# Routing scratch moved out of the logits' bank, first queries loaded by halves, and weight splits moved between engines in a retention and mixture-of-experts kernel

## The chip, the cores and the metric

One core of one Trainium2 chip runs the whole program. The metric is device time in microseconds of one execution: the median of three runs. Lower is better. TensorE is called PE below (PEld is its loading of weights), VectorE DVE, ScalarE ACT, GpSimd POOL and SyncE SP.

## What is computed

Attention with a decaying state, for 4 batches, 8 heads, 768 positions and 64 columns a head, feeds a mixture of 8 experts of which each token takes the best one. Cut to what matters:

```python
gamma = 1.0 - 2.0 ** (-5.0 - np.arange(H))
for t in range(S):
    state = gamma[None, :, None, None] * state + np.einsum('bhd,bhe->bhde', k[:, :, t], v[:, :, t])
    y[:, :, t] = scale * np.einsum('bhd,bhde->bhe', q[:, :, t], state)
x = y.transpose(0, 2, 1, 3).reshape(B * S, H * D)             # 3072 tokens of 512
logits = x @ w_gate;  e_idx = np.argmax(logits, axis=1)
gate_w = softmax(logits)[np.arange(N), e_idx]
eom = 1.0 / (1.0 + np.exp(-(x @ w_output_gate)))
for e in range(E):
    mask = e_idx == e
    h = np.maximum(x[mask] @ w1[e], 0.0)                      # 512 -> 1024
    out[mask] = gate_w[mask, None] * eom[mask, e, None] * (h @ w2[e])
```

## The kernel before

The order of the work on every engine is written out by hand (`manual_schedule`), so each engine executes what the program's lines issue to it, in their order; the framework adds only the waits.

**Attention.** The sequences are cut into 24 chunks of 128 positions, and two chunks (of two batches) make a pair `p`, 0 to 11. Within a pair PE makes, in this order: the products with the state (`inter`), the scores of both chunks into four banks of PSUM (`sp[0]` to `sp[3]`, each 128 x 512), the tokens of the chunks two pairs back (`tokens`, into `sp[0]` and `sp[1]`), the turned logits of the pair before, a turn of queries into `sp[0]`, the values into `yp`, the new state into `st`, the turned keys of the next pair (`turn_keys`, into `sp[2]` and `sp[3]`), the `counts` of the pair before, a second turn of queries into `sp[1]`, and the `logits` of this pair into `misc`. DVE masks the scores, scales the outputs into `yt` and does the small operations of the routing; ACT copies keys, queries, state and logits out of PSUM (`keep_keys`, `keep_queries`, `keep_logits`), takes exponentials and makes the output rows (`rows_out`); POOL scales the values (`prep_v`) and scatters the rows to the experts' regions in memory (`srt`). Loads run on SP's queue.

**Routing.** `route1` (eight DVE operations) gets the best expert `oh` from the turned logits, `exps` its exponentials, `counts` (five small products) how many tokens of each expert came earlier, `route2` the row number `pos` and `gates` the factor `gate`, by which `rows_out` multiplies two pairs later. The counts stand in `misc[:, 2 * P:]` and the scratch of all these steps in `small`, a part of the same bank; the logits of the pair are written to `misc[:, 0:2 * P]`.

**Start.** Queries are loaded for two chunks at once (`load_q`, 512 KB, rows of both parities side by side), parted by a copy for each parity (`part_queries`), turned, and copied to `qt`. `warm_up` gives PE products that nobody reads. The tables `gn` and `ga` of the decay and the values of chunk 0 go over ACT's queue, the four pieces of the gate weights `wg` over SP's.

**Head.** The expert with most tokens is chosen from pair 7 on; its first 256 rows are computed early, as a stream of 192 products (`head_all`: stage 1 of tile 0, then stage 1 of tile f and stage 2 of tile f - 1, twelve each, for eight tiles). `run_head(n)` puts the next n of them into PE's order. Weights are split into a high and a low part for each tile: `split_high` (two ACT casts), `split_low` (two halves, the first on DVE and the second on POOL unless said otherwise). `head_prep` turns and splits the first rows. At the end of the stream stands `begin_x0`, which takes the expert's remaining rows; they are loaded (`load_x`) when the last scatter and a clearing of unused rows (`clear`) have landed.

**Experts.** From there on PE runs the eight experts, with their weights loaded, split and used in a row of 64 tiles.

Of the kernel before, what the change touches and what calls it, by code (L numbers as in the profile page):

```python
# [10 lines left out]
F32 = mybir.dt.float32  # L11
# [22 lines left out]
def retention_moe_kernel(  # L34
# [167 lines left out]

    def split_weights(s: int):
        split_high(s)
        split_low(s)
# [25 lines left out]
    with ExitStack() as actx:  # L231
# [59 lines left out]
        load_q(0, 0)  # L291
        load_k(0)
        nc.scalar.activation(warm, warm, AF.Exp)
        nc.scalar.dma_start(gv, dec_v)
        load_v(0, nc.scalar)
        for o in range(2):
            nc.scalar.dma_start(gn[rows(o)].rearrange("p (b s) t -> p b (s t)", b=2),
                                dec_q[:, 2 * o * P:2 * o * P + 2 * P].unsqueeze(0).broadcast_to([HP, 2, 2 * P]))
        nc.scalar.dma_start(ga.rearrange("p b c g -> p (b c g)"),
                            dec_c.rearrange("b x -> (b x)").unsqueeze(0).broadcast_to([P, 2 * NC * NG]))  # L300
        load_k(1)
        load_q(1, 0)
        load_v(1)
        load_k(2)
        load_k(3)
        load_v(2)
        for o in range(2):
            for x, w in ((0, w_gate), (E, w_ogate)):
                nc.sync.dma_start(wg[rows(o), :, x:x + E],
                                  w[o * DM // 2:(o + 1) * DM // 2].rearrange("(g p) e -> p g e", p=HP))  # L310
        load_v(3)
        load_q(0, 1)

# [23 lines left out]
        def turn_queries(ch, j, r, bank):  # L337
            src = qr.pop((ch, j, r))
            for g in range(NG):
                nc.tensor.transpose(blocks(bank)[:, g], src[:, 2 * g:2 * g + 2].rearrange("p h d -> p (h d)"), ident)  # L340

# [183 lines left out]
        def totals(n):  # L525
            tot = (misc[:, 0:E] if n < NCH else st[:, 0, 2 * E:3 * E])
# [43 lines left out]
        def head_stage1(f):  # L570
# [3 lines left out]
            for r, ls, dcs in [(r, ls, g) for g in ((0, 1), (2, 3)) for r, ls in (("xh", (hi, lo)), ("xl", (hi,)))]:  # L574
                for dc in dcs:
                    for l in ls:
# [3 lines left out]
                        yield  # L580
# [4 lines left out]
            hd["h", f] = h  # L585

# [51 lines left out]
        constants_first()  # L638
        prep_v(0)
# [3 lines left out]
        warm_up(misc, 12)  # L643
        for r, eng in enumerate((nc.vector, nc.scalar)):
            part_queries(0, 0, r, eng)
        for r, eng in enumerate((nc.vector, nc.scalar)):
            turn_queries(0, 0, r, yp[r])
# [563 lines left out]
```

## Time and profile before

| | us |
|---|---|
| median of three runs | 436.72 (436.64 to 436.79) |
| the profiled execution | 437.49 |
| its span in the trace | 435.8 |
| PE busy, of the span | 406.2 (93%) |
| PEld busy | 379.2 (87%) |
| POOL busy | 254.2 (58%) |
| DVE busy | 227.8 (52%) |
| ACT busy | 186.9 (43%) |

The span runs from the first to the last instruction on the chip; the execution's own time has 1.7 us more around it. The profile records each instruction with its engine, line and tiles, what it waited for, and the clock that was granted to PE. Shares of the whole span mix stages with different limits: the attention (to about 140 us), the head (to 169) and the experts.

### The profile page before, as it was taken

To read this page: it belongs to the slowest core of one execution; us is meant where nothing else is said; L and a number is where in the kernel's file an instruction comes from. 1 tells how busy PE (TensorE), PEld (TensorE's weight loads), DVE (VectorE), ACT (ScalarE), POOL (GpSimd) and SP (SyncE) were. 2 spreads that over 40 slices of the span, in tenths; PEclk is the share of its full clock that TensorE was granted. 3 is DMA by queue.
4 is the path that set the end of the run, shared out by engine and by line. 5 is a ranking of instruction groups with operands and counts; after the bars stand their busy time and mean duration, and the time that the engine had idled before them with its cause. 6 is when DMAs were issued, how large, how long until landed. Compare 5 with 4: busy or idle time off the path is not lost.

```text
span 435.8 us, 10454 instructions
## 1 busy us (share of the span) xinstructions
PE 406.2 (93%) x3600; PEld 379.2 (87%) x3600; DVE 227.8 (52%) x563; ACT 186.9 (43%) x360; POOL 254.2 (58%) x301
## 2 busy tenths in 40 slices
PE   7989999999988699999999999999999999999991
PEld 3767777777776699999999999999999999999881
DVE  4455556565687575673544455355265366354110
ACT  3355544555553423563543444354354454353010
POOL 1636564444466212788246677777776877884712
PEclk9999999999999699999999999999999999999997
DMA  9898777878734559679749549658748848840102
GB/s 229 198 247 231 193 189 213 219 188 238 215 107 148 170 147 183 198 212 221 180 149 206 165 133 218 186 164 187 204 142 196 226 150 195 231 126 9 51 16 71
DMA packets 128380, 75.74 MB, mean 174 GB/s; under 512 B 57748, under 2 KB 116504, under 8 KB 128288
## 3 DMA queue, kind: packets, MB, share of 16 engines
q1 hardware_dynamic: 120896, 59.15, 54.7%
q0 software_dynamic: 5776, 14.76, 9.6%
q8 instruction: 61, 1.00, 1.0%
q10 hardware_dynamic: 1616, 0.57, 0.5%
q14 instruction: 31, 0.25, 0.2%
HBM read 59.71 MB, written 15.30 MB: 172 GB/s over the span
## 4 chain that ended last, share of the span: by engine, by line
PE 81%; POOL 5%; issue 4%; DMA 3%; DVE 3%; ACT 2%; SPq 0%; ACTq 0%; DVEq 0%; POOLq 0%
PE h L937 28%; PE a L960 26%; PE y L386 5%; PE s L368 4%; PE s L595 3%; PE s L327 2%; PE s L497 2%; PE y L577 2%; PE st L393 2%; PE y L360 2%; POOL out_dram L208 2%; DMA kn<-in_k_dram 2%; DMA qn<-in_q_dram 1%; PE a L988 1%; PE s L340 1%
## 5 line engine op out<-in xcount | busy, mean ns | idle before, releaser
L201 POOL TENSOR_TENSOR wlo<-raw,whi 128x512 fp32r<-128x512 f32 x59 | 79.1, 1342 | 47.0 <-ACT whi L193 32.8
L208 POOL DMA_INDIRECT out_dram<-ot,idi x85 | 84.9, 999 | 22.4 <-issue 17.2
L937 PE MATMUL h<-xh,whi 128*128 128x360 f32 (+5 forms) x256 | 84.3, 329 | 0.2 <-issue 0.2
L937 PE MATMUL h<-xw,whi 128*128 128x360 f32 (+5 forms) x256 | 84.3, 329 | 0.0
L937 PE MATMUL h<-xh,wlo 128*128 128x360 f32 (+5 forms) x256 | 84.1, 329 | 0.0
L947 DVE SCALAR_TENSOR_TENSOR hl<-h,hh 128x192 fp32r<-128x192 f32 (+7 forms) x64 | 35.4, 553 | 83.3 <-ACT hh L946 83.1
L960 PE MATMUL a<-hh,whi 128*128 128x392 f32 (+4 forms) x224 | 73.8, 329 | 0.0
L960 PE MATMUL a<-hl,whi 128*128 128x392 f32 (+4 forms) x224 | 73.7, 329 | 0.0
L960 PE MATMUL a<-hh,wlo 128*128 128x392 f32 (+4 forms) x224 | 73.5, 328 | 0.0
L946 ACT ACTIVATE hh<-h 128x192 fp32r<-128x192 f32 (+7 forms) x64 | 31.3, 489 | 73.9 <-PE h L937 72.8
L200 DVE TENSOR_TENSOR wlo<-raw,whi 128x512 fp32r<-128x512 f32 x64 | 46.2, 722 | 28.7 <-ACT whi L192 23.1
L192 ACT CAST whi<-raw 128x512 fp32r<-128x512 f32 x64 | 39.6, 618 | 36.3 <-PE a L960 26.3
L513 POOL DMA_INDIRECT srt<-row,pos x24 | 24.2, 1009 | 45.7 <-ACT row L504 42.6
L937 PEld LDWEIGHTS h<-xh,whi 128*128 128x128 f32 x256 | 48.3, 188 | 1.1 <-issue 0.5
L937 PEld LDWEIGHTS h<-xw,whi 128*128 128x128 f32 x256 | 48.2, 188 | 0.6
L937 PEld LDWEIGHTS h<-xh,wlo 128*128 128x128 f32 x256 | 48.2, 188 | 0.2
L376 DVE TENSOR_TENSOR am<-s,mask 128x512 f32<-128x512 f32 x48 | 29.9, 683 | 27.6 <-PE s L368 27.6
L960 PEld LDWEIGHTS a<-hh,whi 128*128 128x128 f32 x224 | 42.2, 188 | 0.2
L960 PEld LDWEIGHTS a<-hh,wlo 128*128 128x128 f32 x224 | 42.2, 188 | 0.2
L960 PEld LDWEIGHTS a<-hl,whi 128*128 128x128 f32 x224 | 42.2, 188 | 0.2
L193 ACT CAST whi<-raw 128x512 fp32r<-128x512 f32 x64 | 39.5, 617 | 0.0
L317 POOL TENSOR_TENSOR vs<-vn,gv 128x512 f32<-128x512 f32 x24 | 24.5, 1041 | 11.4 <-DMA vn<-in_v_dram 8.3
(186 smaller groups left out, 628.6 us busy)
## 6 DMA issues: line engine op xcount, KB each, us to landing
raw<-in_moe_w_dram SPq DMA_DIRECT2D x128, 128.0 KB
raw<-in_moe_w_dram SPq DMA_DIRECT2D x64, 256.0 KB
qn<-in_q_dram SPq DMA_DIRECT2D x12, 512.0 KB
kn<-in_k_dram SPq DMA_DIRECT2D x24, 256.0 KB
vn<-in_v_dram SPq DMA_DIRECT2D x23, 256.0 KB
xl<-srt SPq DMA_DIRECT2D x12, 209.6 KB
xl<-srt SPq DMA_DIRECT2D x8, 225.8 KB
xl<-srt SPq DMA_DIRECT2D x8, 193.5 KB
```

The costliest lines, as they stand in the source:

```text
L192: nc.scalar.copy(hi[:, 0], raw[:, 0])
L193: nc.scalar.copy(perm(hi), r2)
L200: (first or nc.vector).tensor_sub(lo[:, 0], raw[:, 0], hi[:, 0].bitcast(F32))
L201: (second or nc.gpsimd).tensor_sub(perm(lo), r2, perm(hi).bitcast(F32))
L208: st = nc.gpsimd.indirect_dma_start(out=dst, out_offset=bass.IndirectOffsetOnAxis(ap=idx, axis=0), in_=src, in_offset=None, bounds_check=n ...
L317: nc.gpsimd.tensor_mul(vs[i], vn.pop(i), gv[:, c, :].unsqueeze(2).broadcast_to([P, H, D]))
L376: nc.vector.tensor_tensor(out=a.rearrange("p s o t -> p (s o) t"), in0=sp[2 * (n % 2) + b].rearrange("p (x t) -> p x t", t=P), in1=mask.un ...
L513: s_ = nc.gpsimd.indirect_dma_start(out=srt, out_offset=bass.IndirectOffsetOnAxis(ap=rt.pop(("pos", i)), axis=0), in_=row.rearrange("p a x ...
L937: nc.tensor.matmul(ps[:, 0:C], l[:, 0, w], r[:, dc, 0:C], start=(n == 0), stop=(n == 3 * NDC - 1))
L946: nc.scalar.activation(hh, ps[:, 0:C], AF.Relu)
L947: nc.vector.scalar_tensor_tensor(out=hl, in0=ps[:, 0:C], scalar=0.0, in1=hh.bitcast(F32), op0=ALU.max, op1=ALU.subtract)
L960: nc.tensor.matmul(accs[d][:, 0:C], l[:, 1, w], r[:, 0:C], start=(f == 0 and n == 0), stop=(f == NF - 1 and n == 2))
```

## The change

**Counts, row numbers and gates.** `counts`, `route2` and `gates` take a bank as an argument: `sp[0]`, in the last pair `sp[3]`, and behind the last pair `st`. They stand in front of the turned keys. Pair 1's queries of the second pair of batches are turned behind the keys.

**First queries.** The first queries of both batches are loaded in halves (64 partitions, 256 KB each) and turned straight from the loaded tile in eight blocks of 64 columns, without the copies of the parts: the first halves ahead of the first scores, the second halves behind them. Nine warm-up products remain of 12 + 2.

**Queues.** `gn` and `ga` go over POOL's queue, `wg` over ACT's, the values of chunk 0 over SP's.

**Splits.** New helpers `low_first` and `low_second` make one half of a low part each. Tiles 0 and 1 have both halves on POOL, tile 2 the first on DVE and the second on POOL, tile 3 both on DVE; high parts move by up to a pair. Both `head_prep` stand at the end of pair 10.

**Last pair.** The tokens of pair 10 are turned ahead of the first 12 head products, and products of the head are spread over the routing of pair 11. `head_stage1` issues its activation and low part with its last product, and no longer with the next product behind it.

```diff
+        def first_queries(ch, o):
+            if o == 0:
+                q0[ch] = ap.tile([P, 2, H, D], F32, name="qn", tag="qn", bufs=2)
+            nc.sync.dma_start(q0[ch][rows(o)],
+                              q[ch, :, o * P:o * P + P, :].rearrange("h (p r) d -> p r h d", r=2))
+        first_queries(0, 0)
         load_k(0)
+        first_queries(1, 0)
+        load_k(1)
         nc.scalar.activation(warm, warm, AF.Exp)
         nc.scalar.dma_start(gv, dec_v)
-        load_v(0, nc.scalar)
...
+        def turn_first(ch, o, bank):
+            for r in range(2):
+                for g in range(NG):
+                    nc.tensor.transpose(bank.rearrange("p (g r t) -> p g r t", g=NG, r=2)[:, g, r],
+                                        q0[ch][rows(o), r, 2 * g:2 * g + 2].rearrange("p h d -> p (h d)"),
+                                        ident[rows(o), o * HP:o * HP + HP])
...
-        def counts(grp, last=False):
+        def counts(grp, bank):
...
-            cnt = st[:, 0, 0:n * E] if last else misc[:, 2 * P:2 * P + n * E]
+            cnt = bank[:, 0:n * E]
...
-        def route2(grp):
+        def route2(grp, bank):
...
-            rk = small[:, 8 * E:10 * E].rearrange("p (a e) -> p a e", a=2)
+            rk = bank[:, 4 * E:6 * E].rearrange("p (a e) -> p a e", a=2)
...
-        warm_up(misc, 12)
...
+        warm_up(misc, 9)
+        turn_first(0, 0, yp[0])
+        keep_first(0, 0, yp[0], nc.vector)
+        turn_keys(0, yp[1])
+        keep_keys(0, yp[1])
+        turn_first(1, 0, st.rearrange("p a x -> p (a x)"))
+        keep_first(1, 0, st.rearrange("p a x -> p (a x)"), nc.vector)
+        turn_keys(1, sp[2])
+        keep_keys(1, sp[2])
...
+            if p == 0:
+                for ch in range(2):
+                    turn_first(ch, 1, sp[ch])
+                    keep_first(ch, 1, sp[ch], nc.scalar)
...
+            if grp:
+                bank = sp[3 if last else 0]
+                counts(grp, bank)
+                add_counts(grp, nc.gpsimd)
+                route2(grp, bank)
+                gates(grp, bank[:, 6 * E:6 * E + 4])
             if n0 + 2 < NCH:
                 turn_keys(n0 + 2, sp[2])
                 keep_keys(n0 + 2, sp[2])
                 turn_keys(n0 + 3, sp[3])
                 keep_keys(n0 + 3, sp[3])
-            if grp:
-                counts(grp)
-                add_counts(grp, nc.gpsimd)
-                route2(grp)
-                gates(grp, small[:, 10 * E:10 * E + 4])
+            if p == 1:
+                for r in range(2):
+                    turn_queries(1, 1, r, sp[r])
+                    keep_queries(1, 1, r, sp[r])
...
-        for i in group(NCH // 2 - 2):
-            tokens(i)
-            rows_out(i)
-            scatter(i)
+        run_head(5)
         turn_logits(grp)
         route1(grp)
         exps(grp)
+        run_head(7)
+        split_high(4)
+        run_head(8)
+        counts(grp, st[:, 0])
+        add_counts(grp, nc.vector)
+        route2(grp, st[:, 0])
+        gates(grp, st[:, 0, 6 * E:6 * E + 4])
+        low_first(3, nc.vector)
+        low_second(3, nc.vector)
         head_ids()
-        split_low(NF - 5, None, nc.vector)
-        split_high(NF - 4)
-        split_high(NF - 3)
-        run_head(15)
-        counts(grp, True)
```

Three places show how instructions move. First PE, from the state of a middle pair to its logits, before (`kn` keys, `oh` the chosen experts, `qr` queries, `yt` outputs, `s_124` to `s_127` the score banks):

```order
L393 MATMUL st<-vs,kn 64x64 x16
L327 MATMUL s_126<-ident,kn 128x128 x4
L327 MATMUL s_127<-ident,kn 128x128 x4
L459 LDWEIGHTS tri_b
L459 MATMUL misc<-oh,tri_b 128x16
...
L464 MATMUL misc<-oh,ones_b 128x8
L340 MATMUL s_125<-ident,qr 128x128 x4
L412 MATMUL misc<-yt,wg 32x256 x4
```

and now:

```order
L418 MATMUL st<-vs,kn 64x64 x16
L484 LDWEIGHTS tri_b
L484 MATMUL s_124<-oh,tri_b 128x16
...
L489 MATMUL s_124<-oh,ones_b 128x8
L340 MATMUL s_126<-ident,kn 128x128 x4
L340 MATMUL s_127<-ident,kn 128x128 x4
L353 MATMUL s_125<-ident,qr 128x128 x4
L437 MATMUL misc<-yt,wg 32x256 x4
```

The counts moved in front of the turned keys and write `s_124` (`sp[0]`); the logits alone write `misc` here.

Second ACT, from the exponentials of pair 11's routing round to the first rows behind it, before (`lt` logits, `row` output rows, `whi` high parts of weights, `h` the head's activations):

```order
L451 ACTIVATE ex<-misc 128x18
L417 COPY lt<-misc 128x256
L504 ACTIVATE row<-s_124,gate 128x4x4x32
L504 ACTIVATE row<-s_125,gate 128x4x4x32
L451 ACTIVATE ex<-misc 128x18
L192 CAST whi<-raw 128x512
L193 CAST whi<-raw 128x4x4x32
L192 CAST whi<-raw 128x512
L193 CAST whi<-raw 128x4x4x32
L582 ACTIVATE h_2290<-s_126 128x256
L582 ACTIVATE h_2305<-y_129 128x256
```

and now:

```order
L476 ACTIVATE ex<-misc 128x18
L608 ACTIVATE h_2239<-s_126 128x256
L529 ACTIVATE row<-s_124,gate 128x4x4x32
L442 COPY lt<-misc 128x256
L529 ACTIVATE row<-s_125,gate 128x4x4x32
L476 ACTIVATE ex<-misc 128x18
L608 ACTIVATE h_2295<-y_129 128x256
L192 CAST whi<-raw 128x512
L193 CAST whi<-raw 128x4x4x32
```

Both activations of `h` moved in front of the casts, and the copy of the logits stands between the two rows.

Third SP's queue at the start, before (`qn` queries, `kn` keys, `vn` values, `wg` gate weights):

```order
L267 DMA qn<-in_q_dram 128x8x128
L257 DMA kn<-in_k_dram 128x8x64 x2
L267 DMA qn<-in_q_dram 128x8x128
L262 DMA vn<-in_v_dram 128x8x64
L257 DMA kn<-in_k_dram 128x8x64 x2
L262 DMA vn<-in_v_dram 128x8x64
L309 DMA wg<-in_moe_w_gate_dram 64x4x8
```

and now:

```order
L303 DMA qn<-in_q_dram 64x16x64
L264 DMA kn<-in_k_dram 128x8x64
L303 DMA qn<-in_q_dram 64x16x64
L264 DMA kn<-in_k_dram 128x8x64
L269 DMA vn<-in_v_dram 128x8x64 x2
L303 DMA qn<-in_q_dram 64x16x64 x2
L264 DMA kn<-in_k_dram 128x8x64 x2
L269 DMA vn<-in_v_dram 128x8x64 x2
L274 DMA qn<-in_q_dram 128x8x128 x2
```

Half loads of queries alternate with the keys, and the gate weights are gone from this queue.

## Rows read from the trace of the kernel before

**Rows 1.** Stretches: us; busy of PE, PEld, DVE, ACT, POOL; clock, DMA share, GB/s.

```profile
40.00:110.00 70.00, 63.43 (x1021) 53.19 (x1020) 40.85 (x135) 35.53 (x71) 35.11 (x69) 1.00 0.80 208
...
170.00:420.00 250.00, 249.83 (x1476) 245.85 (x1475) 124.69 (x241) 106.65 (x203) 173.87 (x155) 1.00 0.64 167
```

**Rows 2.** Waits of PE, whole span: us in total, times, longest.

```profile
PE misc L412 <- DVE gate L488: 9.4, 10, 1.4
PE s L595 <- DVE h L583: 4.1, 1, 4.1
...
PE s L340 <- ACT qr L323: 1.1, 1, 1.1
PE misc L459 <- ACT ex L451: 1.1, 1, 1.1
```

**Rows 3.** Timeline, pair 9: start, us, engine, line, operation [idle before <-releaser].

```profile
113.03 1.29 DVE L403 TENSOR_TENSOR yt<-y,gq 128x512 f32<-128x512 f32 x2
...
114.28 1.09 PE L327 MATMUL s<-ident,kn 128*128 128x128 f32 x8
...
115.34 0.64 PE L340 MATMUL s<-ident,qr 128*128 128x128 f32 x4
...
115.60 0.18 DVE L473 TENSOR_TENSOR misc<-misc,oh 128x16 f32<-128x16 f32 x1 [1.28 <-PE misc L464]
...
116.64 0.17 DVE L488 RECIPROCAL gate<-misc 128x2 f32<-128x2 f32 x1
...
116.87 0.64 PE L412 MATMUL misc<-yt,wg 128*32 128x256 f32 x8 [0.89 <-DVE gate L488]
```

**Rows 4.** Chain that ended last, behind the last pair: start, us, what.

```profile
141.97 0.06 ACT whi L192
...
144.93 1.01 PE s L595 x3
...
148.42 0.64 PE s L595 x3
...
166.41 2.88 PE s L595 x24
```

**Rows 5.** Stretches of 1 us behind the last pair.

```profile
144.00:145.00 1.00, 0.07 (x1) 0.07 (x1) 0.55 (x2) 0.69 (x3) 0.00 (x0) 0.58 0.97 287
...
151.00:152.00 1.00, 1.00 (x11) 0.96 (x11) 0.37 (x4) 0.43 (x1) 0.24 (x2) 1.00 0.41 161
```

**Rows 6.** Costliest groups of the page: | busy us, mean ns | idle before.

```profile
L376 DVE TENSOR_TENSOR am<-s,mask 128x512 f32<-128x512 f32 x48 | 29.9, 683 | 27.6 <-PE s L368 27.6
...
L201 POOL TENSOR_TENSOR wlo<-raw,whi 128x512 fp32r<-128x512 f32 x59 | 79.1, 1342 | 47.0 <-ACT whi L193 32.8
```

**Rows 7.** Timeline of the start, TensorE.

```profile
8.87 0.66 PE L327 MATMUL s<-ident,kn 128*128 128x128 f32 x4 [1.81 <-DMA kn<-in_k_dram]
...
13.18 1.16 PE L368 MATMUL s<-qt,kt 64*128 64x128 f32 x16 [1.02 <-DVE qt L323]
...
14.28 2.07 PE L386 MATMUL y<-am,vs 128*64 128x128 f32 x32
```

**Rows 8.** Two stretches of the start.

```profile
3.00:13.00 10.00, 7.32 (x51) 4.48 (x49) 4.59 (x9) 3.00 (x5) 2.70 (x5) 1.00 1.22 301
...
13.50:15.50 2.00, 2.00 (x38) 1.85 (x36) 1.15 (x2) 0.00 (x0) 0.26 (x1) 1.00 0.32 31
```

**Rows 9.** Timeline of SyncE's queue, the last gate table.

```profile
13.27 0.61 SPq L309 DMA_DIRECT2D wg<-n_moe_w_output_gate_dram  x1
```

**Rows 10.** Timeline, GpSimd and VectorE: two clearings, the head's second rows.

```profile
154.12 1.49 POOL L217 DMA_INDIRECT srt<-zrow,endr  x1 [0.93 <-DVE endr L819]
...
163.69 0.97 POOL L217 DMA_INDIRECT srt<-zrow,endr  x1 [8.07 <-DMA xl<-srt]
...
167.47 1.16 DVE L894 STREAM_TRANSPOSE xt<-xl 128x192 f32<-128x192 f32 x4 [0.17 <-issue]
```

More of the change, by code (lines that the diff above doesn't have):

```diff
@@ L306, in retention_moe_kernel @@
         load_v(2)
[L307 to L310, printed above, removed]
         load_v(3)
         load_q(0, 1)
+        load_q(1, 1)
         def prep_v(i):
@@ L525, in totals @@
         def totals(n):
-            tot = (misc[:, 0:E] if n < NCH else st[:, 0, 2 * E:3 * E])
+            tot = (misc[:, 0:E] if n < NCH else st[:, 0, 7 * E:8 * E])
             for a in range(2):
@@ L638, in retention_moe_kernel @@
         constants_first()
+        for o in range(2):
+            nc.gpsimd.dma_start(gn[rows(o)].rearrange("p (b s) t -> p b (s t)", b=2),
+                                dec_q[:, 2 * o * P:2 * o * P + 2 * P].unsqueeze(0).broadcast_to([HP, 2, 2 * P]))
+        nc.gpsimd.dma_start(ga.rearrange("p b c g -> p (b c g)"),
+                            dec_c.rearrange("b x -> (b x)").unsqueeze(0).broadcast_to([P, 2 * NC * NG]))
+        warm_up(misc, 9)
[7 more added lines that the diff above has]
+        keep_keys(1, sp[2])
         prep_v(0)
@@ L658, in retention_moe_kernel @@
             grp = group(p - 1)
+            nxt = p + 1
+            ahead = (p % 2, p // 2 + 1) if 2 <= p < 2 * NQ - 2 else None
+            last = p == NCH // 2 - 1
             if n0 + 4 < NCH:
@@ L662, in retention_moe_kernel @@
                 load_v(n0 + 4)
-            nxt = p + 1
-            ahead = (p % 2, p // 2 + 1) if 1 <= p < 2 * NQ - 2 else None
-            if nxt // 2 + 1 < NQ:
+            if p > 0 and nxt // 2 + 1 < NQ:
                 load_q(nxt % 2, nxt // 2 + 1)
@@ L694, in retention_moe_kernel @@
                     rows_out(i)
-                    scatter(i)
+                    if not last:
+                        scatter(i)
             if grp:
@@ L712, in retention_moe_kernel @@
                 keep_queries(*ahead, 0, sp[0])
-            if p == LOAD_AT + 1:
-                head_prep(1)
+            if p == 10:
+                split_high(1)
+            if last:
+                split_high(3)
+                low_second(2, nc.gpsimd)
+                for i in (n0 - 4, n0 - 3):
+                    scatter(i)
             if grp:
@@ L748, in retention_moe_kernel @@
                 keep_queries(*ahead, 1, sp[1])
-            if p == NCH // 2 - 1:
+            if last:
+                for i in (n0 - 2, n0 - 1):
+                    tokens(i)
                 run_head(12)
+                rows_out(n0 - 2)
+                scatter(n0 - 2)
             logits(group(p))
             keep_logits(group(p))
+            if last:
+                rows_out(n0 - 1)
+                scatter(n0 - 1)
             for i in (n0 + 2, n0 + 3):
@@ L757, in retention_moe_kernel @@
                 more_gq(p + 1)
-            if nxt // 2 + 1 < NQ:
+            if nxt >= 2 and nxt // 2 + 1 < NQ:
                 for r in range(2):
-                    if p == 0:
-                        part_queries(0, 1, r)
-                    else:
-                        part_queries(nxt % 2, nxt // 2 + 1, r)
+                    part_queries(nxt % 2, nxt // 2 + 1, r)
             if p == 0:
+                for r in range(2):
+                    part_queries(0, 1, r)
                 constants_second()
```

66 lines of the change are left out of this document (30 added, 36 removed).

## The prediction

> **What bounds the kernel now.** I read first the busy time by stretches [rows 1]: from 170 to 420 us TensorE (PE) is busy for 249.83 of 250 us, so nothing can be won there, and whatever comes earlier moves the end by as much. From 40 to 110 us it is busy for 63.43 of 70: the attention pairs leave it idle for 0.94 us in ten. Second, the list of what PE waited for [rows 2]. Ten waits of the logits for `gate` on VectorE (DVE) make 9.4 us, one wait of the head's second stage for `h` makes 4.1, and the others are near 1 us each. Third, the timeline of one pair [rows 3], for what a wait of the logits consists of: PE turns keys (114.28), counts, turns queries (115.34, 0.64 us) and is then free, but the logits start only at 116.87. They overwrite `misc`, and the counts, the row numbers and the gates' scratch lie in that bank, so six small DVE operations, from 115.60 to 116.81, must end first. Those could not start sooner, as the counts stand behind two key turns: DVE idled 1.28 us for them, while the outputs (113.03, 1.29 us) had ended at 114.32. Last, the chain that ended last, around 145 us [rows 4], and the granted clock there [rows 5].
>
> **Pairs 2 to 10.** The counts now go to bank `sp[0]` and stand ahead of the key turns. In the pair of rows 3 they would run when the state ends, at 114.28, and push the keys back by the 0.1 us that they cost behind them before. The DVE chain of 1.21 us begins when the outputs end, 114.3, and ends near 115.6. The logits need `yt`, ready at 114.32, and no longer the gates; PE reaches them when the queries' turn ends, 115.34 + 0.64 = 115.98. So 0.89 us go and no wait takes their place: the next writer of `sp[0]` is the next pair's scores, behind logits of 0.64 us and the products with the state, so after 116.6, when the gates are done. Ten waits of 9.4 us, less one tenth for pair 1: **8.5 us**. The cover is that the counts find `oh` ready, which DVE makes ahead of the outputs, thus before 113.03; without it PE would wait at the counts, for what `oh` is late. What is late next in a pair is the queries' bank, which a row copy on ScalarE (ACT) frees; nothing changes there.
>
> **Pair 1.** Queries (1, 1) were turned ahead of the values and waited 1.1 us for their load [rows 2]; now they are turned behind the keys. Their own work only moves. The masks, 4 x 0.683 us behind the scores [rows 6], keep the values back by an estimated 0.3 of this. As these queries turn into `sp[0]`, they wait for the gates, an estimated 0.45 us in place of the logits' 0.89. 1.1 - 0.3 + 0.44 = 1.2, of which I take **1.1 us**.
>
> **The start.** The values of pair 0 begin at 14.28 [rows 7]. The second keys came at 8.87, when five loads (queries 0.52, keys 0.26, values 0.26, `gn` 0.26, keys 0.26 MB) were in: 1.57 MB at 301 GB/s [rows 8] take 5.2 us, so the stream starts in effect at 3.65. Now 1.05 MB (two halves of queries, two chunks of keys) and `gn` come first: 3.65 + 1.31/0.301 = 8.0. Then turning keys 0.66, scores 1.16 [rows 7], and four masks: 8.0 + 0.66 + 1.16 + 4 x 0.683 = 12.55. The fourth half of the queries, after 2.36 MB, is there at 11.5; its turn, eight blocks of 64 columns, is at most the 0.66 of four full blocks and ends at 12.2, under the masks. So the values begin near 12.5, an estimate: **1.8 us**. The bounds are -1.7 (rival 3) and 2.3, if `gn` comes in beside the stream. The copies of the parts, on DVE and ACT, and five warm-up products stood in waiting time and cost nothing. The four gate tables leave the queue of SyncE (SP): issuing one took 0.61 us [rows 9], and behind their issue the stream carried 31 GB/s for 2 us [rows 8]. On ACT's queue they end before its first copy. SP takes the values of chunk 0 instead and issues six query loads where there were four. `gn` (two transfers) and `ga` cost GpSimd's (POOL) queue three issues, bounded by 0.97 and 1.49 us, its indirect ones [rows 10]; POOL has nothing else until the first values land. The loads of queries (0, 1) and (1, 1) now wait on SP for the turns of the second halves, and keys and values of chunks 4 and 5 queue behind them; at 12.5 us 3.4 MB have been issued and 2.7 have come, so the stream does not run dry.
>
> Row and rule on the smaller pieces: the loads of the first 13 us hold keys and values in pieces of 256 bytes and ran at 301 GB/s [rows 8], so I charge the halves of queries, now in such pieces too, that rate. The Trainium skill, "DMA: Bandwidth & Descriptors", section Specifications, speaks against this part of the change: it wants at least 512 bytes for line rate. By it the sum would be that of rival 3, 3.5 us less.
>
> **Behind the last pair.** PE stood still for 4.1 us up to 144.93 [rows 2, 4]: stage two of the head needs `h`, whose activation stood on ACT behind four casts of weights (from 141.97), and whose low half stood on DVE behind eight routing operations, the ids and two splits. The granted clock fell during it (0.58 in the microsecond from 144, 1.00 again from 151 [rows 5]), to the 1.2 GHz level: a step of the head took 0.64/3 = 0.213 us in place of 2.88/24 = 0.120 [rows 4]. Of 6.1 us at that level 6.1 x (1 - 0.120/0.213) = 2.7 are lost. The change puts `h` of each tile ahead of the casts on ACT, `h` of tile 0 ahead of the routing on DVE, and gives PE 7 + 8 steps (1.8 us) between the turned logits and the counts. The 1.1 us wait for `ex` [rows 2] came of a DVE transposition ahead of the routing, which moves to the pair before. So 4.1 + 1.1 + 2.7 = 7.9, less an estimated 0.4, as the turned logits now wait for a copy that stands behind a row on ACT: **7.5 us**. The first halves of splits 0 and 1 go from DVE to POOL, at an estimated 1.34 us each, by its second halves [rows 6]; POOL is busy for 35.11 of 70 us [rows 1], so they are hidden. The bounds of this part are 1, if another late input takes the place of `h` and the clock falls too (rival 2), and 8.2. What is late next is the chain of the last scatter, the clearing and the second part of the head's rows: clearing at 154.12, rows in by 163.69, used at 167.47 [rows 10], 3.8 us of slack, of which I expect 2 to be left.
>
> Sum: 1.8 + 1.1 + 8.5 + 7.5 = 18.9 us. The profiled execution took 437.49 us, 0.77 above the median of the runs, 436.72; I take the gain off the median: **417.8 us**, with a range of its own from 415 to 420.
>
> **The rivals.**
> 1. Transfers become the bound of the pairs. They moved 208 GB/s [rows 1]; 70 us less six waits of 0.89 want 225. For it: waits for free buffers leave holes in the stream. Against: 301 GB/s were reached [rows 8], and no pair behind pair 1 waited for a load [rows 2]. At 215 GB/s pairs 2 to 10, some 100 us, would win 3.3 us, not 8.5: 423.0. Chance 0.12.
> 2. Another input is late behind the last pair (split 2, whose halves now lie on two engines, or the head's rows); PE stands again, and the clock falls. For it: ACT and DVE have as much to do as before, and only its order changes. Against: what PE needs there now stands first on each engine. 6.5 of the 7.5 us come back: 424.3. Chance 0.12.
> 3. The half loads of queries run at half the rate, their pieces being half as long and going to 64 partitions: 1.05/0.301 = 3.5 us more, 421.3. Against: the rate of rows 8. The rule of the Trainium skill above is on its side. Chance 0.05.
> 4. The other side: the clock falls at the start. Fourteen warm-up products become nine, and the two ahead of the first scores go; PE then has short turns with waits between until 8.7 us. If the clock falls there and pairs that are 90% busy do not bring it back, the 63.43 us of work between 40 and 110 take up to 0.213/0.120 as long, 49 us more, or 0.7 us for each us; beyond 18.9/0.7 = 27 us of attention at that level the kernel is slower, and with those 70 us at 467. Against: PE waited 1.81 us ahead of 8.87 [rows 7] with no loss shown, and the clock came back in 6 us of unbroken work [rows 5]. Chance 0.03.
> 5. The change doesn't do what it says: the logits still wait for a later DVE instruction than `yt`. Then 8.9 us stay: 426.7. Chance 0.02.
>
> **How the numbers follow.** The forecast has 0.66. It and rivals 1, 2, 3 and 5 are faster by over 0.2% (about what a measurement of this kernel can tell from no change): 0.97, of which 0.01 goes to no change, for several rivals at once. So 0.96 faster, 0.01 the same, 0.03 slower. The range takes in the forecast's own, rivals 1 to 3, and below 415 the upper bounds of start and tail: 414.5 to 424.5.
>
> **What would show it.** Right: no wait of the logits for `gate` from pair 2 on; values of pair 0 near 12.5; no standstill of PE over 1 us behind the last pair, and a granted clock of 1.00 there. Wrong: loads among PE's waits after 30 us (rival 1), a wait for `wlo`, `xw` or `h` of over 2 us behind the last pair (rival 2), a granted clock of 0.50 before 40 us (rival 4).

## The result, and the profile after

The changed kernel takes 421.1 us (median of 4 runs, 419.97 to 423.51) against 436.68 in the same comparison: a ratio of 0.9657, interval 0.961 to 0.9704, so 15.6 us less. The forecast was 18.9 us less, 417.8; the time lies in the range of 414.5 to 424.5, in its upper half, and above the 415 to 420 that the forecast gave itself without its rivals. Ratios, here and below, are of fast runs alone, as a kernel has a second, slower state in some of its runs; so a ratio can differ from the quotient of the medians beside it. The profiled execution has a span of 419.6 us against 435.8.

To see where the 16.2 us of span come from, take one event per stage that both kernels have: the start of the logits of a pair (line 412 before, 437 now), and the first product of the first expert pass (937, 985). Of the kernel before, the timeline of TensorE (start, duration, engine, line, operation, and in brackets the idle time before it):

```profile
18.23 0.64 PE L412 MATMUL misc<-yt,wg 128*32 128x256 f32 x8
30.27 0.64 PE L412 MATMUL misc<-yt,wg 128*32 128x256 f32 x8 [0.89 <-DVE gate L488]
...
127.22 0.64 PE L412 MATMUL misc<-yt,wg 128*32 128x256 f32 x8 [1.38 <-DVE gate L488]
137.55 0.64 PE L412 MATMUL misc<-yt,wg 128*32 128x256 f32 x8
...
169.13 0.25 PE L937 MATMUL h<-xh,whi 128*128 128x192 f32 x1
```

And of the changed kernel, the same view, with the start and pair 9 beside these events:

```profile
8.45 0.71 PE L358 MATMUL st<-ident,qn 64*128 64x64 f32 x8 [1.58 <-DMA qn<-in_q_dram]
...
9.80 3.53 PE L393 MATMUL s<-qt,kt 64*128 64x128 f32 x32
...
14.85 1.97 PE L411 MATMUL y<-am,vs 128*64 128x128 f32 x32
...
18.70 0.64 PE L437 MATMUL misc<-yt,wg 128*32 128x256 f32 x8
29.35 0.64 PE L437 MATMUL misc<-yt,wg 128*32 128x256 f32 x8
...
107.73 0.60 PE L353 MATMUL s<-ident,qr 128*128 128x128 f32 x4
108.27 0.64 PE L437 MATMUL misc<-yt,wg 128*32 128x256 f32 x8
...
117.18 0.64 PE L437 MATMUL misc<-yt,wg 128*32 128x256 f32 x8
127.37 0.64 PE L437 MATMUL misc<-yt,wg 128*32 128x256 f32 x8
...
151.97 0.25 PE L985 MATMUL h<-xh,whi 128*128 128x192 f32 x1
```

| stage, by these events | before, us | after, us | gained | forecast |
|---|---|---|---|---|
| to the logits of pair 0 | 18.23 | 18.70 | -0.47 | 1.8 |
| pair 1, to its logits | 12.04 | 10.65 | 1.39 | 1.1 |
| pairs 2 to 10 | 96.95 | 87.83 | 9.12 | 8.5 |
| pair 11 | 10.33 | 10.19 | 0.14 | 0 |
| behind it, to the first expert product | 31.58 | 24.60 | 6.98 | 7.5 |
| first expert product to the end | 266.67 | 267.63 | -0.96 | 0 |
| sum | 435.8 | 419.6 | 16.2 | 18.9 |

**The pairs.** In pair 9 the logits now follow the turned queries at once, where they had waited 0.89 us [rows 3]. The timeline of VectorE shows why: outputs first, the gates ready as the logits begin, and nobody waits for them.

```profile
105.43 1.29 DVE L428 TENSOR_TENSOR yt<-y,gq 128x512 f32<-128x512 f32 x2
107.09 0.18 DVE L498 TENSOR_TENSOR s<-s,oh 128x16 f32<-128x16 f32 x1 [0.36 <-PE s L489]
...
108.20 0.17 DVE L513 RECIPROCAL gate<-s 128x2 f32<-128x2 f32 x1
```

The list of what TensorE waited for (in all, times, longest) has no wait of the logits left and no load behind 30 us; the longest entries of [rows 2] are gone:

```profile
PE st L358 <- DMA qn<-in_q_dram: 1.6, 1, 1.6
...
PE y L411 <- POOL vs L330: 0.6, 1, 0.6
```

**Start and tail.** The stretches (busy time of PE, PEld, DVE, ACT, POOL; granted clock, DMA share, GB/s):

```profile
5.00:8.00 3.00, 1.87 (x13) 1.35 (x12) 0.69 (x1) 0.58 (x1) 0.00 (x0) 1.00 1.19 222
8.00:11.00 3.00, 2.55 (x22) 2.19 (x24) 0.69 (x1) 0.58 (x1) 1.09 (x2) 0.75 1.17 264
...
9.50:13.00 3.50, 3.50 (x33) 3.22 (x33) 1.41 (x3) 0.58 (x1) 2.95 (x5) 0.51 1.13 245
...
40.00:110.00 70.00, 69.36 (x1147) 59.26 (x1145) 44.66 (x149) 39.08 (x80) 37.73 (x74) 1.00 0.88 229
...
140.00:150.00 10.00, 9.91 (x79) 9.43 (x79) 5.42 (x19) 3.82 (x8) 0.00 (x0) 1.00 1.01 225
```

From 40 to 110 us TensorE is busy for 69.36 of 70 where it was 63.43 [rows 1], and the stream moves 229 GB/s. Behind the last pair neither standstill nor low clock is left. But at the start the clock is at its lower level, 1.2 GHz, from 9.5 to 13 us: the 32 score products take 3.53 us, where two times 16 took 1.16 each [rows 7], and the stream is slower than it was. The stretches before at the same place:

```profile
5.00:8.00 3.00, 2.05 (x15) 1.28 (x12) 1.72 (x3) 1.21 (x2) 0.79 (x1) 1.00 1.24 292
8.00:11.00 3.00, 2.13 (x22) 1.55 (x22) 0.43 (x1) 1.19 (x2) 0.25 (x1) 1.00 1.22 314
```

**The end.** Of the 0.96 us lost behind 152 us only 0.10 lie before TensorE's last product (its end came 17.06 us earlier). The rest lies behind the last issue of a write by GpSimd: 7.5 us to the end of the span, 6.7 before. In the profiles of the first four runs below this is 6.0 to 7.7 us, with the same code there, so I count it as spread between executions.

### The profile page after: what moved, and what is told of

Its sections match the earlier page's. It is cut to its first block, busy times and chain, and to the rows that moved or that the text cites. A ratio compares the mean times of both kernels' runs of the same rounds, so it can differ in the third digit from the quotient of the medians.

```text
span 419.6 us, 10492 instructions
## 1 busy us (share of the span) xinstructions
PE 404.4 (96%) x3611; PEld 378.3 (90%) x3611; DVE 222.8 (53%) x557; ACT 185.3 (44%) x360; POOL 257.3 (61%) x306
## 4 chain that ended last, share of the span: by engine, by line
PE 79%; issue 5%; POOL 5%; DMA 5%; DVE 2%; ACT 1%; SPq 1%; POOLq 0%; ACTq 0%; DVEq 0%
PE h L985 29%; PE a L1008 27%; PE y L411 4%; PE s L393 4%; PE s L353 2%; PE st L418 2%; PE y L385 2%; POOL out_dram L215 2%; PE s L340 2%; PE s L522 1%; DMA qn<-in_q_dram 1%; PE s L622 1%; PE a L1036 1%; DMA raw<-in_moe_w_dram 1%; DMA srt<-row,pos 1%
## 5 line engine op out<-in xcount | busy, mean ns | idle before, releaser
L201 POOL TENSOR_TENSOR wlo<-raw,whi 128x512 fp32r<-128x512 f32 x56 | 74.9, 1338 | 44.3 <-ACT whi L193 27.1
L200 DVE TENSOR_TENSOR wlo<-raw,whi 128x512 fp32r<-128x512 f32 x60 | 42.4, 707 | 27.2 <-ACT whi L192 22.9
L927 ACT CAST xh<-xt 128x416 fp32r<-128x416 f32 (+2 forms) x28 | 15.1, 540 | 36.7 <-DVE xt L926 36.7
```

The lines of the kernel that those rows point to most:

```text
L200: (first or nc.vector).tensor_sub(lo[:, 0], raw[:, 0], hi[:, 0].bitcast(F32))
L201: (second or nc.gpsimd).tensor_sub(perm(lo), r2, perm(hi).bitcast(F32))
```

## The experiments

My theory after this reading: pairs and tail work as forecast; the start lost what it should have won, because the clock falls there and its loads come late. The rivals: the parts depend on each other, or the loads alone are to blame. Runs 1 to 4 shared the runs of the kernel before (437.15), runs 5 to 8 those of 437.55; in runs 9 to 11 (447.17) and 12 (446.39) everything was slower, the kernel before too, so there only ratios and the traces count.

### Run 1: the old start

```diff
-        first_queries(0, 0)
-        load_k(0)
-        first_queries(1, 0)
...
+        load_q(0, 0)
+        load_k(0)
...
```

with warm-up products, copies and the places of the first queries as in the kernel before.

> The changed kernel with the start of the kernel before (whole first queries, its queues, 14 warm-up products, queries of pair 1 at their old places). Theory A: the new start lost time, as the granted clock was 0.50 from 9.5 to 13 us in it; with the old start the clock stays 1.00 up to 20 us, the values of pair 0 begin at 14.3 (14.85 in the changed kernel), and the time is 0.3 to 1.0 us below the changed kernel's 421.1, thus 420.1 to 420.8. Theory B: the new start is worth what was forecast, and something else took it back: this run is 1.5 to 2 us slower than the changed kernel, 422.6 to 423.1.

418.85 us, ratio 0.9584 (0.956 to 0.9609). The clock stays 1.00, the values of pair 0 begin at 14.43, the logits of pair 0 at 18.38. So the new start costs time: A holds in kind, though the time lies below A's bounds. Of the 2.25 us against the changed kernel only 0.32 lie at the start (1.41 against the profile of run 5); the first expert product comes at 150.69, 1.28 us earlier, since the logits of pair 11 also come 1.04 earlier: the wait of 0.6 us of the values for GpSimd in the list above is not there. That wait is no matter of the start, as runs 5 and 6 have the new start and do not have it. By its median this is the fastest version that I ran; run 6 below (0.9605) can't be told from it.

### Runs 2, 5 and 6: what holds the start

Run 2 puts six products in TensorE's gap of 1.6 us:

```diff
         keep_keys(0, yp[1])
+        warm_up(misc, 6)
         turn_first(1, 0, st.rearrange("p a x -> p (a x)"))
```

> The changed kernel with six more warm-up products on PE between the turn of the first keys and that of the second queries, where it waits 1.6 us for a load. Theory A (the clock set the start): the clock stays 1.00 from 9 to 14 us, the 32 score products take 2.1 to 2.3 us in place of 3.53, the values of pair 0 begin at 13.4 to 13.8 in place of 14.85, and the time is 1.1 to 1.4 us below the changed kernel's. Theory B (loads set the start): the scores still begin at 9.8, the values still wait until 14.5 or later, and the time is the changed kernel's within 0.3 us.

421.75 us (419.63 to 424.16), 0.9646 (0.9614 to 0.9679). The clock stays 1.00. The timeline of TensorE:

```profile
9.54 2.06 PE L393 MATMUL s<-qt,kt 64*128 64x128 f32 x32
12.62 0.68 PE L358 MATMUL s<-ident,qn 64*128 64x64 f32 x8 [1.03 <-DMA qn<-in_q_dram]
...
14.28 1.97 PE L411 MATMUL y<-am,vs 128*64 128x128 f32 x32
```

Each theory is half right: the scores take 2.06 in place of 3.53 us, as A has it, but the values move by 0.57 only, as TensorE now waits for the second halves of the first queries, turned ahead of the values; and the time can't be told from the changed kernel's (0.9657), as B has it.

Run 5 is the changed kernel again.

> The changed kernel itself, for comparison on the chip of the next three runs. Theory A (the clock falls at the start whenever this kernel runs): the clock is 0.50 for some 3 us between 9 and 14 us again, the values of pair 0 begin after 14.5, and the time is 420.5 to 422. Theory B (the fall was a chance of one execution): the clock stays 1.00 and the values begin at 14.3 or earlier, as in the run with six more products.

421.31 us, 0.9618 (0.9579 to 0.9657). The clock falls again, as A has it, but at 14 us; this time it is the values that pay (from 14.50, with 3.42 us in place of 1.97), and the logits of pair 0 come at 19.79:

```profile
14.00:17.50 3.50, 3.50 (x35) 3.38 (x35) 0.06 (x1) 0.58 (x1) 0.00 (x0) 0.51 1.04 246
```

In both profiles of the changed kernel the clock fell at the start, in none of the kernel before or of those with its start (runs 1, 3, 4, 7, 8, 9).

Run 6 is run 2 with the second halves, which only pair 1 reads, behind the values:

```diff
-            if p == 0:
-                for ch in range(2):
-                    turn_first(ch, 1, sp[ch])
-                    keep_first(ch, 1, sp[ch], nc.scalar)
...
             values(n1)
+            if p == 0:
+                for ch in range(2):
+                    turn_first(ch, 1, sp[ch])
+                    keep_first(ch, 1, sp[ch], nc.scalar)
```

> The changed kernel with the six products in the gap, and the turn of the second halves of the first queries (which only pair 1 uses) moved behind the values of pair 0. Theory A (with the clock held, the values of pair 0 wait for nothing but the turn of these halves, whose load comes late): the values begin at 12.1 to 12.6, when the first values times their gates are there, the logits of pair 0 at 17.2 to 17.6 (18.13 with the six products alone, 18.38 with the old start), and the time is 0.8 to 1.2 us below that of the old start, near 417.8. Theory B (the loads of the keys and values of pair 1 set the pace by then): the logits of pair 0 move, but the values of pair 1 stay at 22.9 or later, and the time is 418.5 to 421.

420.28 us, 0.9605 (0.9568 to 0.9642). The timeline of TensorE:

```profile
9.62 0.63 PE L340 MATMUL s<-ident,kn 128*128 128x128 f32 x4 [0.20 <-DMA kn<-in_k_dram]
10.17 2.06 PE L393 MATMUL s<-qt,kt 64*128 64x128 f32 x32
12.27 2.36 PE L411 MATMUL y<-am,vs 128*64 128x128 f32 x32
14.55 1.20 PE L358 MATMUL s<-ident,qn 64*128 64x64 f32 x16
...
17.79 0.64 PE L437 MATMUL misc<-yt,wg 128*32 128x256 f32 x8
...
283.01 0.34 PE L986 MATMUL h<-xw,whi 128*128 128x392 f32 x1 [1.46 <-issue]
```

The values begin at 12.27, where A wanted them, the logits of pair 0 at 17.79 (A: 17.6 at the latest), the values of pair 1 at 22.65, ahead of B's 22.9, and the first expert product at 150.02, the earliest of all. The whole time misses A and lies in B's bounds: in the experts TensorE waits 1.46 us at 283 us for nothing that the profile shows but its own issue. Run 2 has the same at the same line (1.18 us), run 1 and the changed kernel do not. What it is stays open.

### Runs 3 and 4: the two parts alone

Run 3 is the kernel before with the counts, row numbers and gates in `sp[0]` ahead of the key turns (in the last pair `sp[3]`, behind it `st`), nothing else:

```diff
+            if grp:
+                bank = sp[3 if last else 0]
+                counts(grp, bank)
+                add_counts(grp, nc.gpsimd)
+                route2(grp, bank)
+                gates(grp, bank[:, 6 * E:6 * E + 4])
             if n0 + 2 < NCH:
                 turn_keys(n0 + 2, sp[2])
...
-            if grp:
-                counts(grp)
...
```

> The kernel before with one part of the change alone: counts, row numbers and gates in a score bank, ahead of the turned keys. Theory A: the parts add up; no wait of the logits for the gates is left and the time falls by 8.2 to 9.4 us, to 427.3 to 428.5. Theory B: the gain of the pairs also needs the loads and the queries' new places (transfers become the bound otherwise): the time falls by under 6 us and loads appear among the waits of PE.

431.78 us, 0.9885 (0.9849 to 0.9921): 5.4 us less, below A's bounds, and yet B's loads are not among the waits. Up to pair 10 all is won (logits at 116.81 in place of 127.22). Then VectorE stops. Its timeline, and GpSimd's in a fence of its own:

```profile
118.56 6.09 DVE L200 TENSOR_TENSOR wlo<-raw,whi 128x512 fp32r<-128x512 f32 x1
124.58 2.47 DVE L376 TENSOR_TENSOR am<-s,mask 128x512 f32<-128x512 f32 x4
```

```profile
118.42 2.04 POOL L317 TENSOR_TENSOR vs<-vn,gv 128x512 f32<-128x512 f32 x2
...
124.06 0.64 POOL L506 COPY row<-ids 128x4 int32<-128x4 int32 x1
```

One subtraction, the first half of split 2, 0.69 us elsewhere, takes 6.09: it ends at 124.65, as GpSimd's unbroken row of work ends (124.70). The copy at the end of that row, 0.20 us elsewhere, takes 0.64 beside it. The masks stand behind the subtraction, TensorE stands still for 4.9 us, and its clock falls (0.50 from 124 to 130 us). The same half of split 1, at 117.26, took 0.70.

Run 4 is the other part alone: `h` ahead of the casts, the steps of the head, splits and routing in the new order.

```diff
-        split_low(NF - 5, None, nc.vector)
-        split_high(NF - 4)
-        split_high(NF - 3)
-        run_head(15)
+        run_head(7)
+        split_high(4)
+        run_head(8)
         counts(grp, True)
...
```

> The kernel before with the other part alone: weight splits spread over the engines, the head's products and the routing of the last pairs in the new order. Theory A: no standstill behind the last pair, clock 1.00 there, and the time falls by 6.5 to 7.5 us, to 429.2 to 430.2. Theory B: the new order only works because the pairs end earlier against the loads of weights: a wait for split weights or head rows of over 1 us stays, and the time falls by 3 to 5 us.

429.99 us, 0.9826 (0.9796 to 0.9856): 7.2 us less, as A said. By the events, 6.30 us are won behind pair 11 (25.28 in place of 31.58). The parts alone give 5.37 + 7.16 = 12.5 us; together, in run 1, they give 18.3. So 5.8 us, give or take some 2 by the three intervals, exist only if both are made. (Run 1 also has the new places of pair 1's queries; they are a small part of this at most, as the logits of pair 1 begin at 28.96 there, at 29.00 in run 3 and at 29.43 in run 7.)

### Runs 7 and 8: the held subtraction

Run 7 is run 3 with that subtraction moved behind the last pair's masks, on the same engine:

```diff
-                split_low(2)
+                low_second(2, nc.gpsimd)
                 split_high(3)
+            if last:
+                low_first(2, nc.vector)
```

> The run of the counts alone, with one VectorE instruction moved: the first half of split 2, which took 6.09 us there, goes behind the last pair's masks. Theory A (it was held for as long as GpSimd worked without a break beside it): at its new place it takes 0.7 us; the masks of the last pair begin near 119.5 in place of 124.58, PE does not stand still for 4.9 us ahead of them, the logits of pair 11 begin at 126 to 127 in place of 132.5, and the time falls to 425.5 to 428.5 (431.78 without the move). Theory B (the masks were late for something else, a load of weights or rows): the masks stay later than 122 and the time stays above 430.

429.85 us, 0.9818 (0.9767 to 0.9869). The subtraction takes 0.68 us, the masks begin at 120.04 and the standstill ahead of them is gone, as A said; but the logits of pair 11 come at 129.88, not 127, and the time lies over a microsecond above A's bounds, within its interval. The list of waits shows the next late input, the head's low rows, which GpSimd makes behind two scatters:

```profile
PE s L584 <- POOL xw L569: 3.3, 1, 3.3
```

The wait for `h` behind the last pair is also still there, 3.4 us.

Run 8 goes the other way: run 1, with the first half of split 1 put back on VectorE.

```diff
-                low_first(1, nc.gpsimd)
                 low_second(1, nc.gpsimd)
...
                 head_prep(1)
+                low_first(1, nc.vector)
```

> The changed kernel with the old start (418.85), and one instruction put back: the first half of split 1 on VectorE instead of GpSimd, behind the turned head rows of pair 10 and ahead of the masks of pair 11. Theory A (held while GpSimd works without a break): it takes 5 us or more in place of 0.69, the masks of pair 11 are 5 to 6 us late, PE stands still that long in pair 11 and its clock falls, and the time is 5 to 8 us more: 424 to 427. Theory B (order and load of VectorE alone): it takes 0.7 us and moves the masks by under 1 us, which PE hides; the time stays within 1 us of 418.85.

427.07 us, 0.9768 (0.972 to 0.9815), 8.2 us above run 1. VectorE's timeline, GpSimd's, the longest wait of TensorE, and two stretches:

```profile
118.92 6.96 DVE L204 TENSOR_TENSOR wlo<-raw,whi 128x512 fp32r<-128x512 f32 x1
125.81 2.47 DVE L395 TENSOR_TENSOR am<-s,mask 128x512 f32<-128x512 f32 x4
```

```profile
117.97 1.28 POOL L208 TENSOR_TENSOR wlo<-raw,whi 128x512 fp32r<-128x512 f32 x1
...
124.08 1.25 POOL L208 TENSOR_TENSOR wlo<-raw,whi 128x512 fp32r<-128x512 f32 x1
```

```profile
PE s L516 <- DVE am L395: 5.9, 1, 5.9
```

```profile
122.00:126.00 4.00, 0.00 (x0) 0.00 (x0) 4.00 (x2) 0.00 (x0) 3.33 (x5) 0.77 0.00 0
126.00:130.00 4.00, 3.46 (x22) 3.13 (x24) 3.11 (x8) 2.11 (x4) 0.78 (x1) 0.50 0.47 131
```

A holds. GpSimd's row of work ran there from 117.97 to 125.3; the masks came 6.2 us later than in run 1 (119.59), TensorE stood still and came back at the lower clock. The time lost, 8.2 us by the medians and 8.0 by the ratios, is at the upper end of A's bounds. Runs 7 and 8 move the subtraction; none moves GpSimd's work and leaves the subtraction in place, so that GpSimd is what holds it rests on the two ends that fall together.

### Run 9: what the low clock cost

Run 9 is the kernel before with 16 products that nobody reads in the standstill behind the last pair.

```diff
-        run_head(15)
+        run_head(12)
+        warm_up(yp[1], 16)
+        run_head(3)
```

> The kernel before with 16 products that nobody reads on PE, in the standstill of 4.1 us behind the last pair; the wait for the head's rows itself stays. Theory A (the term of 2.7 us for the half clock in the forecast): the clock stays 1.00 from 140 to 160 us, 24 steps of the head take 2.9 us from the first on, and the time falls by 2.3 to 2.8 us. Theory B (the clock's fall costs little, as other engines set the pace behind the standstill): the clock stays up, but PE waits elsewhere, and the time falls by under 1 us.

446.27 us, ratio 1.0004 (0.9962 to 1.0046): the time does not show A's 2.3 us, which lie outside the interval. The trace shows the term itself. Of the kernel before and of this run, the stretch of the standstill, and this run's timeline (one of the 16 products has no record):

```profile
140.00:160.00 20.00, 15.93 (x115) 15.60 (x114) 13.81 (x55) 7.65 (x17) 6.55 (x8) 0.83 0.46 148
```

```profile
140.00:160.00 20.00, 18.25 (x146) 15.23 (x147) 12.89 (x53) 8.69 (x19) 8.71 (x12) 1.00 0.58 169
```

```profile
146.53 3.40 PE L167 MATMUL y<-wz 128*128 128x512 bf16 x15
```

The clock stays up, and from the logits of pair 11 (143.14) to the first expert product (172.00) it takes 28.86 us against 31.58: 2.72 less, the forecast's 2.7. (The 31.58 are from the profile of the first comparison, in which everything was faster; the kernel before was not profiled in this one.) Behind that, the profiled execution has a wait of 2.9 us in the experts (for issue again), enough to hide the gain there; whether the other executions have it is not known.

### Runs 10 to 12: the stream at the start

Run 10 is run 6 with the gate tables' four loads behind the copy of the second keys; run 11 has three products in place of six as well; run 12 also loads the first two chunks of values on ScalarE's queue (the last lines of the diff).

```diff
-        for o in range(2):
-            for x, w in ((0, w_gate), (E, w_ogate)):
-                nc.scalar.dma_start(wg[rows(o), :, x:x + E],
...
         keep_keys(1, sp[2])
+        for o in range(2):
+            for x, w in ((0, w_gate), (E, w_ogate)):
+                nc.scalar.dma_start(wg[rows(o), :, x:x + E],
...
-        load_v(0)
-        load_v(1)
+        load_v(0, nc.scalar)
+        load_v(1, nc.scalar)
```

> The run with the second halves later, with one thing moved: the four gate tables, 64 rows of 32 bytes to a piece, go on ScalarE's queue behind the copy of the second keys in place of the start. Theory A (their small packets slowed the stream from 5 to 8 us, 222 GB/s in place of 292): the rate there is back at 270 or more, the second queries are turned before 8.3, the logits of pair 0 begin at 17.2 to 17.5 (17.79), and the head's end and all behind comes 0.3 to 0.6 us earlier. Theory B (something else slows the stream, the half-width pieces of the queries or the tables that GpSimd loads): the rate stays below 240 and nothing moves by more than 0.2 us.

> The run before this one with three products in the gap of the start in place of six. Theory A (the clock holds as long as the gap is mostly filled): clock 1.00 up to 20 us and the same times as with six, within 0.3 us, but for the instruction that PE waited 1.2 to 1.5 us for at 283 us in the two runs with six, which may lie elsewhere. Theory B: the clock falls to 0.50 between 9 and 18 us again, as in the changed kernel, and the time is 1 us or more above that with six.

> The run with three products and later tables, with the loads of the first two chunks of values on ScalarE's queue in place of SyncE's, so that two hardware queues feed the stream as in the kernel before. Theory A (pieces of 256 bytes cost the stream its rate, whichever queue issues them): from 5 to 11 us it stays at 250 GB/s or less, where the old start has 291 to 307, and the logits of pair 0 begin within 0.4 us of 17.5. Theory B (one queue alone can't feed the stream): the rate from 5 to 8 us is 275 or more, the second queries are turned before 8.0 in place of 8.28, and the logits of pair 0 begin before 17.2. Either way, on a chip where the kernel before takes about 437, the time is 417 to 420, and the clock is 1.00 up to 20 us.

Run 10: 0.9684 (0.9638 to 0.9731). From 5 to 8 us the stream moves 207 GB/s, as B has it: the gate tables are not what slows it. The logits of pair 0 begin at 17.52, 0.27 us earlier, between the two theories. Run 11: 0.9645 (0.9598 to 0.9692), clock 1.00 up to 20 us, logits at 17.53: A holds, three products are enough here. Its wait for issue in the experts is 0.9 us, as run 10's, so the number of products does not decide it. By the ratio neither is faster than run 6 (0.9605); both profiles also wait 2.7 us for `hh` in the experts. Run 12: 0.9761 (0.9725 to 0.9797), slower than both, by neither theory: 265 GB/s from 5 to 8 us lie between their bounds, and the clock of 1.00 that both had expected is not there. What moved is whose bytes come first. TensorE's timeline, and the queues from 5 to 8 us (packets, MB, share of the engines; q10 is ScalarE's, q1 SyncE's):

```profile
10.74 1.11 PE L354 MATMUL st<-ident,qn 64*128 64x64 f32 x8 [2.64 <-DMA qn<-in_q_dram]
...
13.21 3.62 PE L389 MATMUL s<-qt,kt 64*128 64x128 f32 x32
```

```profile
q10 hardware_dynamic: 1583, 0.40, 58.8%
...
q1 hardware_dynamic: 530, 0.13, 19.6%
```

ScalarE's queue, with the values that are not needed yet, took 0.40 MB of the stream, SyncE's with the queries and keys got 0.13; the second queries came at 10.74 in place of 8.28, and in this longer gap the clock fell again: it is 0.53 from 9.5 to 13 us, and the scores at 13.21 take 3.62 us.

## Why the prediction was right, and where it was not

The time lies in the range, because the two large terms held and the small ones missed by less than the range allowed. The range had been widened for rivals 1 to 3; none of them came as foretold, and the start used most of it up: 2.3 of the 2.7 us of span that are missing.

1. **Pairs 2 to 10**, forecast 8.5, measured 9.12. The mechanism is the one foretold: no wait for the gates, DVE's chain beside the key turns, and transfers that followed (229 GB/s from 40 to 110 us, no load waited for), which ends rival 1; rival 5 falls with the list of waits.
2. **Pair 1**, forecast 1.1, measured 1.39, but for another reason than most of that term: run 3, which leaves the queries at their old place, needs 10.66 us from the logits of pair 0 to those of pair 1, run 1 with the new place 10.58. The counts win most of it; the moved queries are worth 0.1 by these two, and 0.6 by run 7, which also leaves them and needs 11.16.
3. **Behind the last pair**, forecast 7.5, measured 6.98. The standstill, the wait for `ex` and the low clock are gone; run 4 has 6.30 us of it alone, run 9 shows the clock's share, 2.72 by the events. Rival 2 did not come in the changed kernel. Run 7 shows that it was near: with the pairs shortened and the old order of this part, the head's low rows are 3.3 us late.
4. **A step costed at nothing decides.** The forecast moved the first halves of splits 0 and 1 to GpSimd and called them "hidden", by GpSimd's busy share. That they are hidden is right. What it left out is what such a half costs on VectorE beside GpSimd's work: that of split 1, put back on VectorE behind the turned head rows, costs 8 us (run 8; at its old place ahead of them it took 0.70 us in run 3), and that of split 2, which the change moves behind the last masks, takes 6.09 us without that move, so that the time falls by 5.4 us only (run 3). VectorE's timeline of before had a sign of it that I passed over; two such subtractions took 1.58 and 1.07 us in place of 0.69:

```profile
127.08 1.58 DVE L200 TENSOR_TENSOR wlo<-raw,whi 128x512 fp32r<-128x512 f32 x1
...
129.28 1.07 DVE L200 TENSOR_TENSOR wlo<-raw,whi 128x512 fp32r<-128x512 f32 x1
```

   The Trainium skill, "SBUF — State Buffer", section "SBUF: two separate sides", says that VectorE and GpSimd share one pair of ports as an exclusive lock, taken for a whole instruction, and that a VectorE instruction with two inputs in SBUF is one that it blocks, against a GpSimd instruction that reads SBUF. The traces agree that it blocks, but go further: the loser waited through several GpSimd instructions in a row (five in run 3), not for one. In run 1 the masks (one input in PSUM; four in 2.48 us from 119.59) and in run 8 the transposes of head rows (one input; four in 1.43 us) ran beside GpSimd's work unhindered.
5. **The start**, forecast 1.8, measured -0.47: the step that failed. No term of the sum stood for the clock; rival 4 had the mechanism, but only as a case in which the clock stays down. Its sign, a granted clock of 0.50 before 40 us, appeared (0.51 from 9.5 to 13 us), and the sign for the forecast, values of pair 0 near 12.5, did not (14.85). The clock came back by 13 us, and cost 0.57 us at the values (14.85 against 14.28 in run 2), in run 5 1.45 us (3.42 against 1.97). The second error: the turn of the second halves "ends at 12.2, under the masks"; with the clock held TensorE waited for their load until 12.62 and 13.67. Run 6 takes both away, and the values begin at 12.27, near the forecast's 12.5. That agreement is luck, as two errors cancel: the second keys are turned at 9.62, where the forecast had them in at 8.0, and the values begin when the scores end, where the forecast put four masks of 2.73 us in between; VectorE made these from 11.43 to 13.91, beside the scores and the values. Even so only 0.44 us of the 1.8 arrive at the logits of pair 0 (17.79 against 18.23), because the turn of the second halves, 1.2 us, still stands in the pair.
6. **The rate of the half loads.** The forecast charged 301 GB/s; measured were 222 and 264 where the old start had 292 and 314. From 8 to 11 us, the packets before and after:

```profile
DMA packets 2780, 0.94 MB, mean 314 GB/s; under 512 B 1792, under 2 KB 2780, under 8 KB 2780
```

```profile
DMA packets 3141, 0.79 MB, mean 264 GB/s; under 512 B 3141, under 2 KB 3141, under 8 KB 3141
```

More packets, fewer bytes: 251 bytes each in place of 338. That is rival 3's direction, and that of the rule of at least 512 bytes in the Trainium skill, "DMA: Bandwidth & Descriptors", section Specifications; the trace agrees that shorter pieces came with a lower rate, but by 16 to 24%, not by half. The section gives no rate for shorter pieces; the half was the forecast's own figure. The number of queues is not the cause from 8 to 11 us, where SyncE's queue moved 0.92 of the 0.94 MB before and all of the 0.79 MB after. No run kept the order of the loads and changed their pieces alone, and the halves also go to 64 partitions in place of 128, so this cause is argued, not shown; run 10 excludes the gate tables.

7. **The end**, forecast 0, measured -0.96: mostly the spread of the last writes (first section).

## What to carry to other kernels

Before an instruction is called hidden on one of two engines, look in the trace for its longest instance, not its mean: an instruction that takes twice its usual time beside a busy neighbour (1.58 us here) can take nearly as long as the neighbour's unbroken row of work (6.09 and 6.96 us), once a change closes the gaps. Test parts of a change alone as well as taken away: here some 5.8 of 18.3 us belong to neither part. At a start, load in the order of first use on few queues, turn what is needed later behind what is needed now, and fill TensorE's gaps; a saved load is worth little if the clock pays for it.

## What the runs showed of the hardware that I had not expected

- A VectorE subtraction of two SBUF inputs, 0.69 us alone, was held for 6.09 and 6.96 us (runs 3, 8), to within 0.6 us of the end of an unbroken row of GpSimd's work.
- TensorE's clock fell to its lower level at the start of the changed kernel at 9.5 us in one execution and at 14 us in another. Before the first fall, from the ninth product's end at 5.3 us, TensorE made only turns, with a gap of 1.58 us; before the second it had made the scores at the higher level up to 11.7 us, then only turns, with gaps of 0.78 and 0.58 us. With three more products in the gap it stayed up (run 11); in run 12, with three products and a gap of 2.64 us behind them, it fell.
- A second queue raised the stream from 237 to 265 GB/s from 5 to 8 us and cost time, because it served what was needed later (run 12 against run 11, from two comparisons).
- TensorE waited 1.46, 1.18, 0.91, 0.93 and 0.92 us for its own issue at one line of the experts in runs 6, 2, 10, 11 and 12, which have the same experts as the changed kernel. The cause was not tried.
